# Scratch layout of split queries and keys in a fused attention block: each hi and lo row stored once, and a head's operand put together by two loads in place of one

## Chip, cores, metric

One NeuronCore of a Trainium2 chip. The metric is the device time of one execution, in microseconds (us); several executions are measured, and the median counts.

## What is computed

A block of a transformer with conditioned layer norm (adaLN), batch 1, S = 2048 tokens, D = 512, H = 32 heads of 16 dims, hidden width F = 1792, all in fp32:

```python
mod = (silu(c) @ w_mod).reshape(1, 6, 1, 512)          # sa, ca, ga, sb, cb, gb
h = layernorm(x) * (1 + ca) + sa
q, k, v = split(h @ wqkv)                              # 32 heads of 16
p = softmax(einsum("bhqd,bhkd->bhqk", q, k) * 16**-0.5)
x = x + ga * ((p @ v) @ wo)
h = layernorm(x) * (1 + cb) + sb
t = h @ w1 + b1
out = x + gb * ((t * tanh(softplus(t))) @ w2)          # Dense, Mish, Dense
```

## The kernel before

**Split products.** TensorE (PE) multiplies in a reduced fp32 form, so a number a is kept as hi(a), rounded, and lo(a) = a − hi(a), and a product is made as hi·hi + lo·hi + hi·lo. For the scores this sum is made by the contraction itself: a head has 16 dims, and each dim takes three rows, q rows (hi, hi, lo) against k rows (hi, lo, hi). That is 48 rows, and two more carry the negated row maximum of the softmax, in two parts, so a head's operand has 50 rows for q and 48 for k and lies in a field of 64 partitions. Two heads (a *pair*) share one buffer: head 0 on partitions 0 to 63, head 1 on 64 to 127. There are NR = 5 buffers `qa` [128, 512] and NR = 5 buffers `ka` [128, 2048], used in turn: pair pp takes buffer pp % 5.

**Scratch.** The q and k units (`qk_unit`) compute 128 columns of q or k (8 heads) for 512 tokens, split them into `qh` and `ql` (in the first stage on ACT and DVE, later on GpSimd, lines L98 and L101), and store both into DRAM: `kscr` [32 heads, 48, 2048] and `qscr` [32, 50, 2048], in the very row order that the operand has. So a hi row is stored twice: for q by two of three transfers of 256 KB (L272), for k by one transfer of 512 KB (L276) beside one of 256 KB for the low rows (L277). The two rows for the maximum are zeros from `constants()`. A pair's loads are then one transfer for each head: `load_q` (L313) reads 50 consecutive rows of 2 KB, `load_k` (L322) 48 rows of 8 KB. Pairs 0 and 1, which come first, take 48 rows of q, and k in pieces of 512 tokens.

**Attention.** 4 blocks of 512 queries times 8 groups of 4 heads are 32 iterations n; an iteration has pairs 2n and 2n+1 and 16 steps of 128 keys. A step has 4 score products (L588) with their exponentials on ACT (L591), 8 products p·v (L606), 4 products for the maxima (L539), each reduced on DVE (L541), and parts of other work: the remaining q, k and v units and later the second half of the block (L139, L132). The maxima of iteration n run 20 steps ahead of its scores; the first ones, before there are scores, run at L553 and L555 while qkv is still being made. When those of an iteration are done, `max_rows` turns them (L568), splits them into `mt` on DVE (L571), and four small transfers (L577, `qa<-mt`) put them into rows 48 and 49 of the heads' `qa`; the first score of that iteration waits for them. At an iteration's end the sums of the softmax go to another layout (L631, `sm<-ot`), DVE takes their reciprocals (L641), and these go out to DRAM and come back spread over partitions (L642, L644); four more transfers move the heads' outputs (L635).

**Order.** The order of all engines is written out by the program. A step t has two half steps, numbered h = 2t and 2t+1, and `at(h, f)` puts f there. Pairs 2 and 3 are loaded at h = −22 and −8, pair 4 at h = 17; from then on odd pairs 2n+1 at 32(n−1), which is 8 half steps ahead of their first maximum, and even ones earlier, at 32(n−2) and 2, 9 or 15 more (the first for n = 3, 4, 5 and 7). All transfers are issued by one engine, SyncE (SP), strictly in program order; each one, beside the waits for its data, waits until the transfer issued eight before it has landed (eight completion counters, DMAHW0 to DMAHW7, taken in turn). So at most eight are under way, and a transfer that waits holds up all behind it.

Of the kernel before, what the change touches and what calls it, by code (L numbers as in the profile page):

```python
# [8 lines left out]
F32 = mybir.dt.float32  # L9
# [9 lines left out]
def adaln_block(ctx: ExitStack, tc: tile.TileContext, x, wqkv, wo, w1, b1, w2, c, w_mod, out):  # L19
    nc = tc.nc  # L20
    P = 128
    S, D = x.shape[1], x.shape[2]
    F = w1.shape[1]
    H = 32
    DH = D // H
    DK = D // P
    FT = F // P
    TB = 512
# [25 lines left out]
    dram = ctx.enter_context(tc.tile_pool(name="dram", bufs=1, space=DRAM))  # L54
    ps = ctx.enter_context(tc.tile_pool(name="ps", bufs=1, space=PSUM))

    kscr = dram.tile([H, 48, S], F32, name="kscr")
    qscr = dram.tile([H, 50, S], F32, name="qscr")
    vscr = dram.tile([G, P, VROW], F32, name="vscr")
    woscr = dram.tile([DK, P, 2, D], F32, name="woscr")  # L60
    w1scr = dram.tile([FT, P, 2, D], F32, name="w1scr")
# [27 lines left out]
    def dap(t, off, ap):  # L89
        return bass.AP(tensor=t.tensor, offset=t.offset + off, ap=ap)  # L90

    def hi_copy(eng, hi, src):
        if eng == "a":
            nc.scalar.copy(hi, src)
        elif eng == "v":
            nc.vector.tensor_copy(hi, src)
        else:
            nc.gpsimd.tensor_scalar(hi, src, 1.0, 0.0, op0=ALU.mult, op1=ALU.add)  # L98

    def lo_sub(eng, lo, src, hi):  # L100
        (nc.gpsimd if eng == "p" else nc.vector).tensor_sub(lo, src, hi.bitcast(F32))  # L101
# [15 lines left out]
    def mm3(acc, ah, al, bh, bl, late="a"):  # L117

        n = len(ah)
        seq = ((ah, bh), (ah, bl), (al, bh)) if late == "a" else ((ah, bh), (al, bh), (ah, bl))  # L120
        seq = [(l[k], r[k]) for l, r in seq for k in range(n)]
        for i, (l, r) in enumerate(seq):
            mm(acc, l, r, i == 0, i == len(seq) - 1)
# [41 lines left out]
    def bank(tag="ms"):  # L165
        return ring() if tag == "ring" else ps.tile([P, TB], F32, tag=tag, name="bk", bufs=1)
# [25 lines left out]
    def clear(h):  # L192

        return h if h < 60 or h % 32 < 25 else h - h % 32 + 34
# [10 lines left out]
    def at(h, f):  # L205

        hooks.setdefault(h, []).append(f)
# [38 lines left out]
    def qk_unit(kind, ct, tb, tag):  # L246

        wh, wl = slices[kind, ct]
        acc = bank(tag)
        ts_ = slice(tb * TB, (tb + 1) * TB)  # L250
        mm3(acc, [wh[:, k, :] for k in range(DK)], [wl[:, k, :] for k in range(DK)],
            [h_h[:, k, ts_] for k in range(DK)], [h_l[:, k, ts_] for k in range(DK)], "b")

        def fin(h=None):
            qh = qp.tile([P, TB], F32R, tag="qh", name="qh", bufs=2)
            ql = qp.tile([P, TB], F32R, tag="ql", name="ql", bufs=2)
            if h is None:
                hi_copy("a", qh, acc)
                lo_sub("v", ql, acc, qh)
            else:  # L260
                qf = pw.tile([P, TB], F32, tag="raw", name="qf", bufs=1)
                nc.scalar.copy(qf, acc)  # L262
                hi_copy("p", qh, qf)
                lo_sub("p", ql, qf, qh)
            scr, rows = (qscr, 50) if kind == 0 else (kscr, 48)

            def put():
                put_away.add((kind, ct, tb))
                o = 8 * ct * rows * S + tb * TB
                if kind == 0:  # L270
                    for r, src in enumerate((qh, qh, ql)):
                        nc.sync.dma_start(dap(scr, o + r * S, [[rows * S, 8], [3 * S, DH], [1, TB]]), src.bitcast(F32))  # L272
                    return
                hi = qh.bitcast(F32)
                twice = bass.AP(tensor=hi.tensor, offset=hi.offset, ap=[list(hi.ap)[0], [0, 2], [1, TB]])
                nc.sync.dma_start(dap(scr, o, [[3 * S, P], [2 * S, 2], [1, TB]]), twice)  # L276
                nc.sync.dma_start(dap(scr, o + S, [[3 * S, P], [1, TB]]), ql.bitcast(F32))  # L277

            put() if h is None else at(clear(h + (5 if h > 60 else 2)), put)
        return fin  # L280
# [25 lines left out]
    def load_q(pp, rows=50):  # L306
        n, j = divmod(pp, 2)
        qb, g = divmod(n, G)
        h = 4 * g + 2 * j
        qt = qa[pp % NR].bitcast(F32)  # L310
        assert (0, h // 8, qb) in put_away, (pp, put_away)
        for s in range(2):
            nc.sync.dma_start(qt[64 * s:64 * s + rows, :], qscr[h + s, :rows, qb * TB:(qb + 1) * TB])  # L313

    def load_k(pp, tb=None):
        n, j = divmod(pp, 2)
        h = 4 * (n % G) + 2 * j
        kt = ka[pp % NR].bitcast(F32)
        at_ = slice(0, S) if tb is None else slice(tb * TB, (tb + 1) * TB)
        assert {(1, h // 8, i) for i in (range(NB) if tb is None else (tb,))} <= put_away, (pp, put_away)  # L320
        for s in range(2):
            nc.sync.dma_start(kt[64 * s:64 * s + 48, at_], kscr[h + s, :, at_])  # L322

    def load_pair(pp):
        load_q(pp)
        load_k(pp)


    with ExitStack() as es:
# [23 lines left out]
        zer = lp.tile([P, TB], F32, name="zer")  # L353
# [113 lines left out]
        apply_tb(1)  # L467
        def constants():
            for q4 in range(S // TB):
                nc.sync.dma_start(dap(qscr, 48 * S + q4 * TB, [[50 * S, H], [S, 2], [1, TB]]), zer[:64, :])  # L470
            nc.sync.dma_start(dap(vscr, VROW - 16, [[VROW, P], [P * VROW, G], [1, 16]]), zer[:, :16 * G])
            nc.sync.dma_start(b1c, b1.rearrange("(f p) -> p f", p=P))

        def unit(fin):
            pe_run()
            fin()

        constants()
        for tb in range(NB):
            if tb + 2 < NB:  # L480
# [27 lines left out]
            if tb == 0:  # L508
                for pp in range(2):
                    load_q(pp, 48)  # L510
            for pp in range(2):
                load_k(pp, tb)
# [7 lines left out]
    ap = ctx.enter_context(tc.tile_pool(name="ap", bufs=1, reuse_waits="tile"))  # L520
# [1029 lines left out]
```

## Time and profile before

| | |
|---|---|
| measured times | 1690.85, 1691.66, 1695.13 us; median 1691.66 |
| profiled execution | 1691.02 us, of it 1689.2 us span of instructions (1.8 around it) |
| busy share | PE 99%, DVE 85%, ACT 80%, GpSimd (POOL) 49% |
| granted TensorE clock | 1.000 |
| transfers | 238.98 MB, mean 141 GB/s |
| share of chain that ended last | PE 91%, DVE 3%, ACT 3%, DMA 2% |

Rows of a timeline give the start and the duration in us, the engine and line, what is written from what (`qa<-qscr`: from qscr into qa), how many neighbours a row gathers (x4), and in brackets the idle time before it and what ended that. An SP row spans the issuing, not the data's way; when the data has landed shows only where somebody waits for it. Rows of the waits give the total in us, the number of times, and the longest. Rows of windows give the busy time of PE, PE's weight loads (PEld), DVE, ACT and POOL with the number of instructions, the granted clock, the share of time in which the 16 DMA engines moved packets, and GB/s.

### The profile page before, as it was taken

To read this page: it belongs to the slowest core of one execution; us is meant where nothing else is said; L and a number is where in the kernel's file an instruction comes from. 1 tells how busy PE (TensorE), PEld (TensorE's weight loads), DVE (VectorE), ACT (ScalarE), POOL (GpSimd) and SP (SyncE) were. 2 spreads that over 40 slices of the span, in tenths; PEclk is the share of its full clock that TensorE was granted. 3 is DMA by queue.
4 is the path that set the end of the run, shared out by engine and by line. 5 is a ranking of instruction groups with operands and counts; after the bars stand their busy time and mean duration, and the time that the engine had idled before them with its cause. 6 is when DMAs were issued, how large, how long until landed. Compare 5 with 4: busy or idle time off the path is not lost.

```text
span 1689.2 us, 33772 instructions
## 1 busy us (share of the span) xinstructions
PE 1667.3 (99%) x12418; PEld 921.5 (55%) x12418; DVE 1441.5 (85%) x2369; ACT 1355.1 (80%) x2612; POOL 821.1 (49%) x843
## 2 busy tenths in 40 slices
PE   7999999999999999999999999999999999999999
PEld 5755655555444455555555455555555455555687
DVE  8898888888989988888889888888889888883377
ACT  6257777777778998888888998888888998889674
POOL 7555224655313564556323564556323565555442
PEclk9999999999999999999999999999999999999999
DMA  7877556777755443434355434534354533533261
GB/s 248 269 244 199 147 150 185 218 223 216 231 142 146 110 94 98 117 88 129 84 137 152 115 77 93 139 77 127 87 144 122 130 94 77 144 107 132 75 230 63
DMA packets 115406, 238.98 MB, mean 141 GB/s; under 512 B 24928, under 2 KB 50544, under 8 KB 109288
## 3 DMA queue, kind: packets, MB, share of 16 engines
q1 hardware_dynamic: 115240, 236.82, 49.9%
q8 instruction: 98, 1.61, 0.4%
q14 instruction: 68, 0.56, 0.1%
HBM read 180.48 MB, written 51.45 MB: 137 GB/s over the span
## 4 chain that ended last, share of the span: by engine, by line
PE 91%; DVE 3%; ACT 3%; DMA 2%; POOL 1%; issue 1%; SPq 0%; ACTq 0%; DVEq 0%; POOLq 0%
PE bk L606 29%; PE ring L588 22%; PE ring L539 20%; PE bk L139 11%; PE bk L132 3%; PE ring L1219 2%; PE ring L132 2%; DVE mx L541 2%; ACT pr L591 1%; PE ring L553 0%; DMA qa<-mt 0%; DMA xt<-in_A_x 0%; PE ring L922 0%; DMA kscr<-qh 0%; PE ring L568 0%
## 5 line engine op out<-in xcount | busy, mean ns | idle before, releaser
L541 DVE TENSOR_REDUCE mx<-ring 128x1 f32<-128x512 f32 x1968 | 1223.1, 682 | 150.0 <-PE ring L539 136.4
L591 ACT ACTIVATE pr<-ring 128x512 f32<-128x512 f32 x2048 | 1078.4, 603 | 207.1 <-PE bk L139 124.7
L539 PE MATMUL ring<-ka,qa 64*128 64x512 f32 x1968 | 817.9, 429 | 1.4 <-ACT pr L591 1.1
L588 PE MATMUL ring<-qa,ka 64*128 64x512 f32 x2048 | 759.1, 402 | 3.4 <-ACT pr L591 1.9
L606 PE MATMUL bk<-pr,vg 128*32 128x512 f32 x4096 | 545.1, 604 | 0.0
L539 PEld LDWEIGHTS ring<-ka,qa 64*128 64x128 f32 x1968 | 350.5, 184 | 326.2 <-DVE mx L541 251.3
L588 PEld LDWEIGHTS ring<-qa,ka 64*128 64x128 f32 x2048 | 373.7, 184 | 194.7 <-DVE mx L541 111.4
L139 PE MATMUL bk<-h,w 64*128 64x512 f32 (+1 forms) x1080 | 278.1, 390 | 0.0
L139 PE MATMUL bk<-w,a_h 64*128 64x512 f32 x632 | 210.9, 413 | 0.0
L139 PEld LDWEIGHTS bk<-h,w 64*128 64x128 f32 x1080 | 178.5, 184 | 9.3 <-ACT pr L591 1.5
L606 PEld LDWEIGHTS bk<-pr,vg 128*32 128x32 f32 x4096 | 81.2, 108 | 135.4 <-issue 126.0
L139 PE MATMUL bk<-w,a_l 64*128 64x512 f32 x316 | 124.0, 392 | 0.0
L139 PEld LDWEIGHTS bk<-w,a_h 64*128 64x128 f32 x632 | 106.8, 184 | 4.3 <-ACT hb L800 1.0
L978 POOL TENSOR_TENSOR y<-yd,y 128x512 f32<-128x512 f32 x44 | 56.9, 1293 | 89.0 <-ACT yd L977 79.7
L812 POOL TENSOR_SCALAR qq<-ee 128x512 f32<-128x512 f32 x25 | 15.5, 619 | 169.6 <-ACT ee L806 169.6
L828 POOL TENSOR_TENSOR qq<-qq,rr 128x512 f32<-128x512 f32 x42 | 54.1, 1289 | 85.9 <-ACT rr L822 85.9
L814 POOL TENSOR_TENSOR hb<-hb,ee 128x512 f32<-128x512 f32 x42 | 54.1, 1288 | 79.6 <-DVE ee L810 77.7
L139 PE MATMUL bk<-w,o_hl 64*128 64x512 f32 x288 | 79.1, 405 | 0.0
L101 POOL TENSOR_TENSOR a_l<-hb,a_h 128x512 fp32r<-128x512 f32 x53 | 73.1, 1379 | 4.4
L98 POOL TENSOR_SCALAR qh<-qf 128x512 fp32r<-128x512 f32 x27 | 16.7, 619 | 90.8 <-ACT qf L262 69.4
L139 PEld LDWEIGHTS bk<-w,a_l 64*128 64x128 f32 x316 | 58.3, 185 | 3.4
L139 PE MATMUL bk<-h_h,wl 64*128 64x512 f32 x168 | 57.2, 420 | 0.2 <-ACT pr L591 0.2
(219 smaller groups left out, 1909.1 us busy)
## 6 DMA issues: line engine op xcount, KB each, us to landing
ka<-kscr SPq DMA_DIRECT2D x124, 384.0 KB
w<-w2scr SPq DMA_DIRECT2D x56, 512.0 KB
w<-w1scr SPq DMA_DIRECT2D x46, 512.0 KB
vg<-vscr SPq DMA_DIRECT2D x32, 552.0 KB
qa<-qscr SPq DMA_DIRECT2D x124, 100.0 KB
kscr<-qh SPq DMA_DIRECT2D x16, 512.0 KB
qscr<-qh SPq DMA_DIRECT2D x32, 256.0 KB
w2scr<-hl SPq DMA_DIRECT2D x14, 512.0 KB
```

What stands on the lines that cost most here:

```text
L101: (nc.gpsimd if eng == "p" else nc.vector).tensor_sub(lo, src, hi.bitcast(F32))
L132: nc.tensor.matmul(acc, l, r, start=start, stop=stop)
L139: i = nc.tensor.matmul(acc, l[64 * g:64 * g + 64], r[64 * g:64 * g + 64], start=start and not then, stop=bool(stop and then))
L539: nc.tensor.matmul(pm, qt[64 * s:64 * s + 64, qs * P:(qs + 1) * P], kt[64 * s:64 * s + 64, kb * TB:(kb + 1) * TB], start=True, stop=True)
L541: nc.vector.tensor_reduce(out=mxs[n][:, s, 4 * j + qs, kb:kb + 1], in_=pm, op=ALU.max, axis=AX.X)
L588: nc.tensor.matmul(p_, kt[64 * s:64 * s + 64, kc * P:(kc + 1) * P], qt[64 * s:64 * s + 64, :], start=True, stop=True)
L591: e = nc.scalar.activation(pr, p_, AF.Exp, scale=SCALE)
L606: nc.tensor.matmul(accs[n][32 * h:32 * h + 32, :], vgs[n][:, o:o + 32], pts.pop((t, h)), start=(kc == 0), stop=(kc == 15))
L814: (nc.vector if tail else nc.gpsimd).tensor_mul(hb, hb, ee)
L828: nc.gpsimd.tensor_mul(qq, qq, rr)
L978: nc.gpsimd.tensor_add(y[i], yd, y[i])
L1219: nc.tensor.matmul(po[i // 2][:, i % 2, :], l[:, s], w[:, r, :], start=(f == 0 and j == 0), stop=(f == FT - 1 and j == 2))
```

## The change

Each hi and each lo row is stored once, two rows for a dim: `kscr` is [32, 32, 2048] and `qscr` [32, 34, 2048] (rows 32 and 33 are the zeros). A unit's stores are two transfers of 256 KB, for q and for k alike. A head's operand is put together by two loads. For q the operand has rows hi (16), then hi and lo in turn (32), then the zeros: the first transfer reads 34 consecutive rows (32 for pairs 0 and 1) to partitions 16 and up, the second the 16 hi rows to partitions 0 to 15. For k the first transfer reads each hi row twice (32 rows), the second the 16 lo rows. What is computed stays the same, and so do the bytes that are loaded; the row order within the contraction differs, for q and k alike.

```diff
-    kscr = dram.tile([H, 48, S], F32, name="kscr")
-    qscr = dram.tile([H, 50, S], F32, name="qscr")
+    kscr = dram.tile([H, 32, S], F32, name="kscr")
+    qscr = dram.tile([H, 34, S], F32, name="qscr")
...
-                if kind == 0:
-                    for r, src in enumerate((qh, qh, ql)):
-                        nc.sync.dma_start(dap(scr, o + r * S, [[rows * S, 8], [3 * S, DH], [1, TB]]), src.bitcast(F32))
-                    return
-                hi = qh.bitcast(F32)
-                twice = bass.AP(tensor=hi.tensor, offset=hi.offset, ap=[list(hi.ap)[0], [0, 2], [1, TB]])
-                nc.sync.dma_start(dap(scr, o, [[3 * S, P], [2 * S, 2], [1, TB]]), twice)
-                nc.sync.dma_start(dap(scr, o + S, [[3 * S, P], [1, TB]]), ql.bitcast(F32))
+                for r, src in enumerate((qh, ql)):
+                    nc.sync.dma_start(dap(scr, o + r * S, [[rows * S, 8], [2 * S, DH], [1, TB]]), src.bitcast(F32))
...
-            nc.sync.dma_start(qt[64 * s:64 * s + rows, :], qscr[h + s, :rows, qb * TB:(qb + 1) * TB])
+            b, o = 64 * s, (h + s) * 34 * S + qb * TB
+            nc.sync.dma_start(qt[b + DH:b + rows, :], dap(qscr, o, [[S, rows - DH], [1, TB]]))
+            nc.sync.dma_start(qt[b:b + DH, :], dap(qscr, o, [[2 * S, DH], [1, TB]]))
...
-            nc.sync.dma_start(kt[64 * s:64 * s + 48, at_], kscr[h + s, :, at_])
+            b, o = 64 * s, (h + s) * 32 * S + at_.start
+            nc.sync.dma_start(kt[b + DH:b + 48, at_], dap(kscr, o, [[2 * S, DH], [0, 2], [1, w]]))
+            nc.sync.dma_start(kt[b:b + DH, at_], dap(kscr, o + S, [[2 * S, DH], [1, w]]))
```

In `constants()` the zeros go to rows 32 and 33. Over the whole program SP issues 1274 transfers in place of 1022: 128 more for q, 140 more for k, 16 fewer stores. The order of the instructions on DVE, ACT and POOL is the same, and so is that of PE, save that the products that start on freshly loaded buffers wait for more completion counters (118 more such waiting instructions). After the stores, line numbers are 2 lower (L575 for L577, L629 for L631, and so on), the loads stand at L308, L309, L319 and L320.

The first place that matters is on SP, ahead of the first four puts of the maxima: the loads of pair 3 and one k unit's stores. Before (`qa_110` and `ka_631` are pair 3's buffers, `qa_107` and `qa_108` those of pairs 0 and 1; in brackets what a row waits for, DMAHW being the completion counters):

```order
L313 DMA qa_110<-qscr 50x512 [waits DMAHW5_49]
L313 DMA qa_110<-qscr 50x512 [waits DMAHW6_49]
L322 DMA ka_631<-kscr 48x2048 [waits DMAHW7_49]
L322 DMA ka_631<-kscr 48x2048 [waits DMAHW0_49]
L276 DMA kscr<-qh 128x2x512 [waits DMAHW1_49,Pool_49]
L277 DMA kscr<-ql 128x512 [waits DMAHW2_49,Pool_49]
L577 DMA qa_107<-mt 2x4x128 [waits DMAHW3_49,DVE_49,PE_49]
L577 DMA qa_108<-mt 2x4x128 [waits DMAHW4_49,PE_49]
```

The same place in the changed program:

```order
L308 DMA qa_110<-qscr 34x512 [waits DMAHW3_49]
L309 DMA qa_110<-qscr 16x512 [waits DMAHW4_49]
L308 DMA qa_110<-qscr 34x512 [waits DMAHW5_49]
L309 DMA qa_110<-qscr 16x512 [waits DMAHW6_49]
L319 DMA ka_650<-kscr 32x1x2048 [waits DMAHW7_49]
L320 DMA ka_650<-kscr 16x2048 [waits DMAHW0_49]
L319 DMA ka_650<-kscr 32x1x2048 [waits DMAHW1_49]
L320 DMA ka_650<-kscr 16x2048 [waits DMAHW2_49]
L271 DMA kscr<-qh 128x512 [waits DMAHW3_49,Pool_49]
L271 DMA kscr<-ql 128x512 [waits DMAHW4_49,Pool_49]
L575 DMA qa_107<-mt 2x4x128 [waits DMAHW5_49,DVE_49,PE_49]
L575 DMA qa_108<-mt 2x4x128 [waits DMAHW6_49,PE_49]
```

The first put stands six rows behind pair 3's first load before and ten behind it now; the load of pair 2, further up, has four more in the same way, and one store of q less lies between. From pair 2's first load to the first put SP has 25 transfers before and 32 now.

The second place is on SP too, at the end of iteration 0: the loads of pair 6, a q unit's stores, a small store, and the transfer of the sums (L631). Before:

```order
L313 DMA qa_108<-qscr 50x512 [waits DMAHW4_49]
L313 DMA qa_108<-qscr 50x512 [waits DMAHW5_49]
L322 DMA ka_106<-kscr 48x2048 [waits DMAHW6_49]
L322 DMA ka_106<-kscr 48x2048 [waits DMAHW7_49]
L272 DMA qscr<-qh 8x16x512 [waits DMAHW0_49,Pool_49]
L272 DMA qscr<-qh 8x16x512 [waits DMAHW1_49]
L272 DMA qscr<-ql 8x16x512 [waits DMAHW2_49,Pool_49]
L730 DMA mscr<-gate_99 4x128 [waits DMAHW3_49,Activation_49]
L631 DMA sm<-ot 128x1x16 [waits DMAHW4_49,Activation_49]
```

And now:

```order
L308 DMA qa_108<-qscr 34x512 [waits DMAHW6_49]
L309 DMA qa_108<-qscr 16x512 [waits DMAHW7_49]
L308 DMA qa_108<-qscr 34x512 [waits DMAHW0_49]
L309 DMA qa_108<-qscr 16x512 [waits DMAHW1_49]
L319 DMA ka_106<-kscr 32x1x2048 [waits DMAHW2_49]
L320 DMA ka_106<-kscr 16x2048 [waits DMAHW3_49]
L319 DMA ka_106<-kscr 32x1x2048 [waits DMAHW4_49]
L320 DMA ka_106<-kscr 16x2048 [waits DMAHW5_49]
L271 DMA qscr<-qh 8x16x512 [waits DMAHW6_49,Pool_49]
L271 DMA qscr<-ql 8x16x512 [waits DMAHW7_49,Pool_49]
L728 DMA mscr<-gate_99 4x128 [waits DMAHW0_49,Activation_49]
L629 DMA sm<-ot 128x1x16 [waits DMAHW1_49,Activation_49]
```

The sums' transfer stood eight rows behind the first load of pair 6 and stands eleven behind it now: four loads more, one store less.

More of the change, by code (lines that the diff above doesn't have):

```diff
@@ L264, in fin @@
                 lo_sub("p", ql, qf, qh)
-            scr, rows = (qscr, 50) if kind == 0 else (kscr, 48)
+            scr, rows = (qscr, 34) if kind == 0 else (kscr, 32)
             def put():
@@ L318, in load_k @@
         kt = ka[pp % NR].bitcast(F32)
-        at_ = slice(0, S) if tb is None else slice(tb * TB, (tb + 1) * TB)
+        at_, w = (slice(0, S), S) if tb is None else (slice(tb * TB, (tb + 1) * TB), TB)
         assert {(1, h // 8, i) for i in (range(NB) if tb is None else (tb,))} <= put_away, (pp, put_away)
         for s in range(2):
-            nc.sync.dma_start(kt[64 * s:64 * s + 48, at_], kscr[h + s, :, at_])
+            b, o = 64 * s, (h + s) * 32 * S + at_.start
+            nc.sync.dma_start(kt[b + DH:b + 48, at_], dap(kscr, o, [[2 * S, DH], [0, 2], [1, w]]))
+            nc.sync.dma_start(kt[b:b + DH, at_], dap(kscr, o + S, [[2 * S, DH], [1, w]]))
     def load_pair(pp):
@@ L469, in constants @@
             for q4 in range(S // TB):
-                nc.sync.dma_start(dap(qscr, 48 * S + q4 * TB, [[50 * S, H], [S, 2], [1, TB]]), zer[:64, :])
+                nc.sync.dma_start(dap(qscr, 32 * S + q4 * TB, [[34 * S, H], [S, 2], [1, TB]]), zer[:64, :])
             nc.sync.dma_start(dap(vscr, VROW - 16, [[VROW, P], [P * VROW, G], [1, 16]]), zer[:, :16 * G])
```

## Prediction

> **What bounds the kernel now.** The page's span, its busy times and its chain come first: they tell which engine a delay must reach before it counts.
>
> ```profile
> span 1689.2 us, 33772 instructions
> PE 1667.3 (99%) x12418; PEld 921.5 (55%) x12418; DVE 1441.5 (85%) x2369; ACT 1355.1 (80%) x2612; POOL 821.1 (49%) x843
> PE 91%; DVE 3%; ACT 3%; DMA 2%; POOL 1%; issue 1%; SPq 0%; ACTq 0%; DVEq 0%; POOLq 0%
> ```
>
> PE is the bound nearly everywhere, so a transfer costs time only where PE, or DVE ahead of it, ends up waiting for it. The waits, asked for PE, show where PE's products now wait for a transfer:
>
> ```profile
> PE ring L588 <- DMA qa<-mt: 1.2, 1, 1.2
> ```
>
> One wait of 1.2 us, for the maxima's put. The change therefore can take away hardly anything, and the question is where it adds. The windows tell how full the transfers' side is (the last two columns: DMA share, GB/s):
>
> ```profile
> 28.00:62.00 34.00, 32.28 (x206) 25.30 (x205) 30.02 (x38) 18.34 (x32) 19.52 (x19) 1.00 0.58 191
> 60.00:70.00 10.00, 10.00 (x73) 8.00 (x72) 9.18 (x9) 1.49 (x4) 4.76 (x6) 1.00 0.92 283
> 80.00:90.00 10.00, 10.00 (x46) 6.18 (x45) 9.24 (x9) 2.17 (x4) 6.53 (x8) 1.00 0.98 340
> 110.00:200.00 90.00, 90.00 (x827) 53.24 (x824) 77.76 (x131) 69.69 (x143) 43.31 (x36) 1.00 0.59 164
> ```
>
> From 60 to 90 us the DMA engines are full (0.92 and 0.98); before that and from 110 on they are at 0.58 and 0.59. That early stage is where more transfers can hurt first. The SP timeline of it:
>
> ```profile
> 71.28 1.19 SPq L313 DMA_DIRECT2D qa<-qscr  x2
> ...
> 88.84 2.49 SPq L313 DMA_DIRECT2D qa<-qscr  x2
> 91.37 1.11 SPq L322 DMA_DIRECT2D ka<-kscr  x2
> ...
> 93.06 0.41 SPq L277 DMA_DIRECT2D kscr<-ql  x1
> 94.67 2.98 SPq L577 DMA_DIRECT2D qa<-mt  x4
> ```
>
> Pair 2 is loaded from 71.28, pair 3 from 88.84, and the first four puts follow from 94.67 to 97.65. PE takes the first score soon after:
>
> ```profile
> 101.88 0.49 PE L588 MATMUL ring<-qa,ka 64*128 64x512 f32 x1
> ```
>
> **The change, part by part.**
>
> *Bytes.* A head's loads still bring 48 rows of k and 50 of q; only stores fall.
>
> ```profile
> DMA packets 115406, 238.98 MB, mean 141 GB/s; under 512 B 24928, under 2 KB 50544, under 8 KB 109288
> ...
> ka<-kscr SPq DMA_DIRECT2D x124, 384.0 KB
> qa<-qscr SPq DMA_DIRECT2D x124, 100.0 KB
> kscr<-qh SPq DMA_DIRECT2D x16, 512.0 KB
> qscr<-qh SPq DMA_DIRECT2D x32, 256.0 KB
> ```
>
> Each of 16 k units and 16 q units stores 256 KB less: 8.4 MB of 238.98. Between 71 and 95 us lie three such units, 768 KB, at the 340 GB/s of the window 2.3 us of transfer time. Whether this comes back is part of A's lower bound.
>
> *A: the first puts.* Between pair 2's first load (71.28) and the first put (94.67) SP has 25 issues now and 32 afterwards: four more for each of two pairs, one store less. SP issues 25 in 23.4 us, 0.94 us each; seven more are 6.6 us. SP had no work from 93.47 (93.06 + 0.41) to 94.67, where the put waited for its data: 1.2 us of slack come off, 5.4 remain. The score at 101.88 comes 4.2 us after the last put left SP (97.65). How long a put takes to land I read where PE did wait for one (the puts on SP's timeline, the score on PE's):
>
> ```profile
> 371.83 3.34 SPq L577 DMA_DIRECT2D qa<-mt  x4
> 380.46 0.47 PE L588 MATMUL ring<-qa,ka 64*128 64x512 f32 x1 [1.24 <-DMA qa<-mt]
> ```
>
> There 5.3 us lay between the last issue (375.17) and the score. So the 4.2 us at the first puts hold no slack worth naming, and I take **+5.5 us**. Upper bound: seven issues at the pace of pair 3's q loads (2.49 / 2 = 1.25), no slack, 8.7. Lower: half-sized transfers free their counters sooner and the seven cost nothing, 0. The pace of pair 2's loads (1.19 / 2 = 0.60) lies between; I stay near 0.94, since it is the mean of this very stretch. PE, full in these windows, can't make the time up.
>
> Why SP is slow there, the waits of its queue show: loads held by earlier stores.
>
> ```profile
> SPq L313 <- DMA qscr<-ql: 10.4, 4, 5.0
> SPq L322 <- DMA kscr<-ql: 6.9, 3, 3.3
> ```
>
> A q store, written as 8 × 16 rows, held it up to 5.0 us, a k store of 128 rows 3.3. [...]
>
> *B: pair 4*, used 12 steps after the first score. The step is the distance of two p·v groups:
>
> ```profile
> 751.41 1.06 PE L606 MATMUL bk<-pr,vg 128*32 128x512 f32 x8
> 754.24 1.06 PE L606 MATMUL bk<-pr,vg 128*32 128x512 f32 x8
> ```
>
> 2.83 us, so at 101.88 + 34.0 = 135.9.
>
> ```profile
> 124.75 0.80 SPq L313 DMA_DIRECT2D qa<-qscr  x2
> 125.59 0.78 SPq L322 DMA_DIRECT2D ka<-kscr  x2
> ```
>
> How long a large transfer takes at worst, the chain shows, in the full stage (start and duration):
>
> ```profile
> 92.58 7.33 DMA kscr<-qh
> ```
>
> Four issues end at 126.4; with 7.33 us to land they are there by 133.7, 2.2 early. Eight issues take 1.6 more, and those ahead of it can bring 1 or 2: **+0.7**, 0 to 2.
>
> *C: the sums of iteration 0*, on SP's timeline, and their reciprocal on DVE's (last row):
>
> ```profile
> 149.43 1.38 SPq L313 DMA_DIRECT2D qa<-qscr  x2
> ...
> 157.35 0.57 SPq L272 DMA_DIRECT2D qscr<-ql  x1
> 160.17 0.52 SPq L730 DMA_DIRECT2D mscr<-gate  x1
> 160.96 0.60 SPq L631 DMA_DIRECT2D sm<-ot  x1
> ...
> 168.19 0.24 DVE L641 RECIPROCAL rc<-sm 128x16 f32<-128x16 f32 x1
> ```
>
> From pair 6's first load (149.43) to the sums (160.96) are 8 issues in 11.5 us, 1.44 each; three more are 4.3. SP sat idle from 157.92 to 160.17, 2.25, which comes off: 2.1. The reciprocal is 6.6 us behind the sums' issue, some of which is slack: **+1.5**, 0 to 4. DVE waits there with all its reductions behind it, and PE for those.
>
> *D: the same in later iterations.* There the sums' transfer waits for ACT, not for a counter:
>
> ```profile
> SPq L631 <- ACT pr L591: 110.3, 26, 7.8
> ```
>
> 26 of the 31 are of this kind, 4.2 us each, more than four issues of an undisturbed load (0.8 / 2 each, row 125.59): mostly covered; **+0.5**, 0 to 2.
>
> *E: the wait at 380*, behind q stores that get fewer: **−0.7**, between 0 and −1.2.
>
> *F: longer waits on PE.* 118 more of these rows:
>
> ```profile
> L539 PEldq EVENT_SEMAPHORE  x122: 51/51/51, 111.8 to 1512.2; - x122
> ```
>
> They exist now from 111.8 on, and from 110 to 200 PE is busy 90.00 of 90 all the same: the wait runs beside the products before it. **0**; without that cover 118 × 51 ns = 6.0 us.
>
> *G: steady loads of odd pairs* are issued four steps, 11.3 us, ahead of use, and later ones with light traffic:
>
> ```profile
> 751.26 0.67 SPq L313 DMA_DIRECT2D qa<-qscr  x2
> 751.98 0.78 SPq L322 DMA_DIRECT2D ka<-kscr  x2
> ```
>
> 1.5 us of issuing become 3.0; with 7.33 landed after 10.3: **0**, covered by 1 us.
> *H: pairs 0 and 1*, loaded ahead of 60 us, k in four pieces of 512 tokens: 20 more issues (4 for q, 16 for k). The groups of first maxima show when the pieces are wanted:
>
> ```profile
> 52.86 0.73 PE L553 MATMUL ring<-ka,qa 64*128 64x512 f32 x4
> ...
> 55.38 0.73 PE L553 MATMUL ring<-ka,qa 64*128 64x512 f32 x4
> ```
>
> A group comes every 2.5 us, 20 of them up to the first score, and the last piece isn't needed by the first twelve, 30 us. 20 issues at 0.4 (row 125.59) are 8 us, spread over 34 us in which the DMA engines stand at 0.58: **0**; if a third fell on the first maximum, 2.7.
>
> Sum: 5.5 + 0.7 + 1.5 + 0.5 − 0.7 = **+7.5 us** (ends, without F and H: −1.2 and +16.7). The span becomes 1696.7, the profiled run 1691.02 + 7.5 = 1698.5. That run lay 0.64 below the median of 1691.66, so for the median I say **1699.2**.
>
> **Rivals.**
>
> *Bytes set the pace, not issues* (ends on the other side: not slower). The engines are at 0.98 and the bytes ahead of the puts fall. If 32 smaller transfers leave as fast as their bytes, the puts go out at 94.67 as before. It decides at a pace of 24.6 / 32 = 0.77 us per issue or less. A is 0, B and C near 0.7 together: −1 to +4, about 1693.7. For it: 283 GB/s at 0.92, so the limit is not the bytes alone but also the packets, whose number in loads stays. Against it: each issue in the timeline waits for one particular landing, and the pair 3 loads took 0.55 to 1.25 each even behind large stores.
>
> *Fewer bytes win.* The wait at 380 goes (1.24) and the 2.3 us of stores come back ahead of the scores: −3.5, 1688.2. Against it: PE is at 10.00 of 10.00 until 90 us, and there is no wait to take away.
>
> *Every odd pair late.* If issue to landing exceeds the 11.3 us (10.3 by G), each of 30 odd pairs holds PE: 1 us late each gives +30, 1729. For it: G's cover is only 1 us. Against it: 7.33 was taken at 340 GB/s, and the whole span's mean is 141.
>
> *The change doesn't do what it says*: the loads move the same bytes with more issues, so for them nothing is saved; this is in the sum.
>
> **How the numbers follow.** Forecast (SP issues bind early, +4 to +17): 0.70. Bytes set the pace: 0.17. Fewer bytes win: 0.05. Odd pairs late: 0.08. From the second case's middle, 1692, to the first case's upper end, 1709, leaves out the fourth, the third and parts of the others, 0.2 together. About 0.3%, 5.1 us, is what a measurement of this kernel can tell from no change: faster is below 1686.6, slower above 1696.7. Slower: 0.65 of the forecast's 0.70, and 0.08: 0.73. Faster: 0.02, the far end of the third case. The same: the rest, 0.25.
>
> **What would show it.** Right: the first score waits for `qa<-mt`, some 5 us, at about 107; the first put leaves SP near 100; near 170 the reciprocal waits for `sm<-ot`; from 200 on the distance of like steps from before stays constant. A wrong: no wait for `qa<-mt` there. G wrong: waits of L539 for `ka<-kscr` in every iteration, and the time above 1709. F wrong: a span longer by some us without any wait for a transfer. Wrong altogether: below 1692, with SP's pace under 0.77 us.

## Result and the profile after

| | before | after |
|---|---|---|
| median of the runs | 1691.26 us | 1714.62 us |
| ratio | | 1.0134, 95% interval 1.0116 to 1.0152 |
| profiled execution, span | 1691.02, 1689.2 us | 1716.85, 1715.0 us |
| granted TensorE clock, mean | 1.000 | 0.993 |

The changed kernel is 23.4 us slower, three times the forecast of 7.5 and beyond its range. Its page, with the granted clock in 40 slices (43 us each):

```profile
span 1715.0 us, 34146 instructions
PE 1674.0 (98%) x12418; PEld 924.4 (54%) x12418; DVE 1442.1 (84%) x2369; ACT 1355.8 (79%) x2612; POOL 822.0 (48%) x843
PEclk9989999999999999999999999999999999999999
PE 85%; DMA 6%; DVE 3%; ACT 2%; SPq 2%; issue 1%; POOL 1%; ACTq 0%; POOLq 0%; DVEq 0%
```

Transfers now hold 6% of the chain that ended last in place of 2%, and the third slice no longer has the full clock. PE's waits show the mechanism that was forecast, and several that were not:

```profile
PE ring L586 <- DMA qa<-mt: 6.5, 2, 5.4
PE ring L586 <- DVE mx L539: 4.4, 3, 2.0
PE ring L551 <- DVE mt L569: 2.0, 1, 2.0
PE ring L537 <- DMA ka<-kscr: 1.5, 1, 1.5
PE bk L132 <- POOL wl L101: 1.3, 1, 1.3
```

Both programs run the same 12418 products in the same order, so the start of each product can be compared one by one. How much later it starts than before, in us (columns: the product's time in the trace of before; "score" is the first score at 101.88 with the product ahead of it; the rows below "after" are experiments told further down):

| | 80 | 95 | ahead of score | score | 120 | 140 | 180 | 350 | 500 | 900 | 1680 |
|---|---|---|---|---|---|---|---|---|---|---|---|
| after | 0.0 | 2.2 | 8.4 | 13.9 | 15.1 | 16.3 | 18.8 | 19.6 | 21.3 | 25.0 | 25.5 |
| 34 + 16 rows on before | 0.0 | 0.0 | 0.3 | 7.6 | 8.9 | 10.1 | 16.7 | 16.9 | 25.5 | 27.4 | 28.6 |
| 32 + 18 rows on before | −0.1 | −0.1 | −0.1 | 1.7 | 3.0 | 3.0 | 3.0 | 3.1 | 4.9 | 5.1 | 6.2 |
| 32 + 18 rows on after | −0.1 | 0.8 | 1.4 | 5.7 | 9.0 | 8.9 | 9.0 | 8.9 | 7.5 | 7.5 | 7.8 |
| 20 tiny transfers on before | 0.0 | 0.0 | 0.0 | 3.1 | 7.4 | 7.3 | 7.4 | 7.5 | 8.2 | 8.1 | 8.1 |

So 15.1 of 25.5 us are lost by 120 us, and the rest in steps. Three things made the first part. SP falls behind before 70 us. Before, four k loads of pairs 0 and 1 and, at the end of that stage, the load of a weight slice stand on its timeline so:

```profile
39.46 1.76 SPq L322 DMA_DIRECT2D ka<-kscr  x4
60.63 0.45 SPq L234 DMA_DIRECT2D wr<-in_A_wqkv  x1
```

After, the first and last of eight, and the weight slice:

```profile
39.55 0.64 SPq L319 DMA_DIRECT2D ka<-kscr  x1
43.97 0.58 SPq L320 DMA_DIRECT2D ka<-kscr  x1
68.77 0.42 SPq L234 DMA_DIRECT2D wr<-in_A_wqkv  x1
```

Eight take 5.0 us (39.55 to 44.55) in place of 1.76: twice as many, and each longer. The weight slice goes out 8.1 us later. GpSimd, which prepares weights from the transfers behind it, waits 9.7 us longer, in two rows of its waits up to 90 us, before and after:

```profile
POOL ep L98 <- DMA ep<-in_B_w: 6.8, 1, 6.8
```

```profile
POOL ep L98 <- DMA ep<-in_B_w: 16.5, 1, 16.5
```

That delay reaches PE at 82 us (`wl`, the row of PE's waits above). Second, from pair 2's first load to the puts:

```profile
80.69 0.72 SPq L308 DMA_DIRECT2D qa<-qscr  x1
102.29 0.30 SPq L308 DMA_DIRECT2D qa<-qscr  x1
112.13 2.86 SPq L575 DMA_DIRECT2D qa<-mt  x4
```

Pair 2 starts 9.4 us late (71.28 before), and its first load to the first put takes 31.4 us for 32 issues, 0.98 each, 8.1 more than before. What SP waited for is in the chain (start, duration):

```profile
81.83 9.63 DMA qa<-qscr
103.01 9.04 DMA qa<-qscr
112.96 2.66 DMA qa<-mt
```

Two of the q loads, 68 KB each, took over 9 us, longer than any large transfer named in the prediction. Third, PE waits, and its clock goes down (the column before the last two):

```profile
115.76 0.76 PE L586 MATMUL ring<-qa,ka 64*128 64x512 f32 x1 [5.43 <-DMA qa<-mt]
```

```profile
95.00:100.00 5.00, 4.12 (x18) 2.43 (x16) 1.52 (x2) 0.10 (x1) 0.00 (x0) 1.00 0.85 263
100.00:105.00 5.00, 2.97 (x7) 1.47 (x8) 4.28 (x5) 1.28 (x3) 3.10 (x4) 0.71 0.79 272
105.00:110.00 5.00, 5.00 (x16) 3.07 (x14) 2.85 (x3) 0.59 (x1) 1.90 (x3) 0.61 0.95 171
110.00:115.00 5.00, 0.33 (x2) 0.00 (x0) 0.10 (x1) 0.00 (x0) 0.24 (x1) 0.73 0.41 120
115.00:120.00 5.00, 3.83 (x17) 2.60 (x19) 3.16 (x5) 2.70 (x5) 2.12 (x3) 0.58 0.71 217
120.00:125.00 5.00, 4.77 (x35) 2.68 (x35) 4.44 (x8) 4.57 (x9) 3.09 (x4) 1.00 1.01 300
```

By finer windows the clock is at 0.50 from 102.1 to 108.9 and from 112.4 to 119.1, and at 1.00 between. The first dip lies ahead of the score and, by the chain above, cost nothing of its own: the put was held by the q load that landed at 112.0, and PE, slow or not, had to wait for the put. Behind the score the distance grows by 1.2 us, from 13.9 to 15.1.

After 120 us the steps come from pair 4's loads (1.1 us), from iterations' ends, where DVE's reciprocal waits for the sums with all reductions behind it, and once from an odd pair's k loads. DVE's timeline at iteration 0 and later, and PE's at 880 us:

```profile
187.29 0.25 DVE L639 RECIPROCAL rc<-sm 128x16 f32<-128x16 f32 x1 [2.68 <-DMA sm<-ot]
375.33 0.25 DVE L639 RECIPROCAL rc<-sm 128x16 f32<-128x16 f32 x1 [2.48 <-DMA sm<-ot]
883.82 0.25 DVE L639 RECIPROCAL rc<-sm 128x16 f32<-128x16 f32 x1 [0.75 <-DMA sm<-ot]
```

```profile
880.09 0.55 PE L537 MATMUL ring<-ka,qa 64*128 64x512 f32 x1 [1.47 <-DMA ka<-kscr]
```

SP's waits name the holder there too: its transfer of the reciprocals, L640, was held 12 times by a q load.

```profile
SPq L640 <- DMA qa<-qscr: 21.1, 12, 3.2
```

### The profile page after: what moved, and what is told of

The parts are those of the page before. It is cut to its first block, busy times and chain, and to the rows that moved or that the text cites. A ratio compares the mean times of both kernels' runs of the same rounds, so it can differ in the third digit from the quotient of the medians.

```text
span 1715.0 us, 34146 instructions
## 1 busy us (share of the span) xinstructions
PE 1674.0 (98%) x12418; PEld 924.4 (54%) x12418; DVE 1442.1 (84%) x2369; ACT 1355.8 (79%) x2612; POOL 822.0 (48%) x843
## 4 chain that ended last, share of the span: by engine, by line
PE 85%; DMA 6%; DVE 3%; ACT 2%; SPq 2%; issue 1%; POOL 1%; ACTq 0%; POOLq 0%; DVEq 0%
PE bk L604 27%; PE ring L586 20%; PE ring L537 18%; PE bk L139 11%; PE ring L1217 2%; DMA qa<-qscr 2%; PE ring L132 2%; DVE mx L539 2%; PE bk L132 2%; ACT pr L589 1%; DMA ka<-kscr 1%; DMA qscr<-qh 1%; DMA qa<-mt 1%; DMA sm<-ot 1%; DMA xt<-in_A_x 0%
## 5 line engine op out<-in xcount | busy, mean ns | idle before, releaser
L586 PE MATMUL ring<-qa,ka 64*128 64x512 f32 x2048 | 761.4, 403 | 13.2 <-DMA qa<-mt 6.5
L586 PEld LDWEIGHTS ring<-qa,ka 64*128 64x128 f32 x2048 | 374.4, 184 | 205.3 <-DVE mx L539 119.1
L139 PEld LDWEIGHTS bk<-h,w 64*128 64x128 f32 x1080 | 178.6, 184 | 10.1 <-ACT pr L589 1.5
L812 POOL TENSOR_TENSOR hb<-hb,ee 128x512 f32<-128x512 f32 x42 | 54.1, 1289 | 79.6 <-DVE ee L808 77.6
```

The costliest lines, as they stand in the source:

```text
L139: i = nc.tensor.matmul(acc, l[64 * g:64 * g + 64], r[64 * g:64 * g + 64], start=start and not then, stop=bool(stop and then))
L586: nc.tensor.matmul(p_, kt[64 * s:64 * s + 64, kc * P:(kc + 1) * P], qt[64 * s:64 * s + 64, :], start=True, stop=True)
L812: (nc.vector if tail else nc.gpsimd).tensor_mul(hb, hb, ee)
```

## Experiments

Two theories: I, the number of SP's issues; R, the rows of the q loads. Changes to time are against the kernel before in the same series.

**34 and 16 rows on the kernel before.**

```diff
-            nc.sync.dma_start(qt[64 * s:64 * s + rows, :], qscr[h + s, :rows, ...])
+            for lo, hi in ((16, rows), (0, 16)):
+                nc.sync.dma_start(qt[64 * s + lo:64 * s + hi, :], qscr[h + s, lo:hi, ...])
```

> The kernel before, its storage and its k loads untouched, with each q load of 50 rows cut into 34 and 16 rows (32 and 16 for pairs 0 and 1). Theory I (the number of transfers that SP issues before the first scores sets the delay): 4 transfers more ahead of 60 us and 4 for pairs 2 and 3, 8 of the 28 less stores that the change adds there, so 2 to 6 us slower, 1694 to 1698. Theory R (a load of 34 rows lands late and holds its completion counter, as the 9.6 and 9.0 us in the changed kernel's chain suggest): most of the change's loss is here already, 12 to 20 us slower, 1704 to 1712, with q loads of pairs 2 and 3 that take 9 us to land.

1716.4 us, ratio 1.0157 (1.0142 to 1.0172): 25.8 slower, more than the whole change (23.4), and beyond what either theory asked for. The wait for the puts is there:

```profile
PE ring L589 <- DMA qa<-mt: 11.2, 3, 7.3
```

The table shows the loss at the first score and again at 180 and 500 us. Theory R stands, if it is the 34 rows and not the 128 further loads (32 and 18 rows, below, decide that). Of theory I this says nothing.

**k loads in two on the kernel before.**

```diff
-            nc.sync.dma_start(kt[64 * s:64 * s + 48, at_], kscr[h + s, :, at_])
+            for lo, hi in ((16, 48), (0, 16)):
+                nc.sync.dma_start(kt[64 * s + lo:64 * s + hi, at_], kscr[h + s, lo:hi, at_])
```

> The kernel before, its storage and its q loads untouched, with each k load of 48 rows cut into 32 and 16 rows. Theory I: 16 transfers more ahead of 60 us, 4 for pairs 2 and 3, so most of the change's loss, 12 to 20 us slower, 1704 to 1712, and pair 2's loads begin some 7 us later than before (71.3 us). Theory R: 0 to 5 us slower, 1691 to 1696.

1703.2, ratio 1.0078 (1.0063 to 1.0093), 12.6 slower, the lower end of what theory I asked for. Pair 2 is loaded from 77.6, 6.3 late. So issues cost too, where no load has 34 rows. The first eight halves on SP's timeline are issued in 0.45 us each, where the change's eight, stepped or with rows repeated, took 0.63:

```profile
39.53 3.61 SPq L323 DMA_DIRECT2D ka<-kscr  x8
```

**The changed kernel without 34-row loads.**

```diff
-    qscr = dram.tile([H, 34, S], F32, name="qscr")
+    qscr = dram.tile([H, 36, S], F32, name="qscr")
...
+            nc.sync.dma_start(qt[b:b + 32, :], dap(qscr, o, [[S, 32], [1, TB]]))
+            nc.sync.dma_start(qt[b + 32:b + rows, :], dap(qscr, o, [[2 * S, rows - 32], [1, TB]]))
...
```

> The changed kernel with the operand's rows in another order, so that a head's q is loaded as 32 rows (hi and lo in turn) and 18 rows (hi, and the two zeros, which lie two rows apart in a field of 36), k as 32 and 16; the number of transfers, their order and nearly all bytes are those of the changed kernel, only no load has 34 rows. Theory I: as slow as the changed kernel, 20 to 25 us above before, 1711 to 1716. Theory R: 12 to 20 us faster than the changed kernel, 1695 to 1703, and pair 2's q loads land within 6 us.

1699.85, ratio 1.0059 (1.0042 to 1.0076): 9.2 above before, 14.8 below the changed kernel's median (14.2 by each one's distance from its own before). The same number of transfers, in the same order. Pair 2's first load, the puts, and the first score:

```profile
80.13 0.80 SPq L308 DMA_DIRECT2D qa<-qscr  x1
102.83 2.84 SPq L575 DMA_DIRECT2D qa<-mt  x4
```

```profile
107.62 0.76 PE L586 MATMUL ring<-qa,ka 64*128 64x512 f32 x1 [4.26 <-DMA qa<-mt]
```

32 issues now take 22.7 us, 0.71 each: less than the 23.4 that 25 took before. So without the 34-row loads the issues of pairs 2 and 3 cost nothing (the prediction's rival "bytes set the pace" had its point at 0.77), and all of the 8.2 us by which the puts are late was there at pair 2's first load, 8.9 late, from the issues ahead of 70 us. Nor does anything come later: the table stands at 9.0 at 120 us, and falls by 1.3 at 380, where the old wait goes, as term E of the prediction had it. Pair 2's q loads had landed within 4.6 us, inside the 6 expected (80.13 to 81.71 on SP's timeline; the transfers eight behind them, which wait for their counters, left at 84.72 to 86.16), and SP's waits for q loads at L640 are nearly gone:

```profile
SPq L640 <- DMA qa<-qscr: 1.3, 1, 1.3
```

**20 tiny transfers on the kernel before.**

```diff
+        nc.sync.dma_start(dmy[i:i + 1, :], x[i:i + 1, :16])   # behind each load of pairs 0 and 1
```

> The kernel before with one transfer of 64 bytes, which nobody waits for, behind each of the 20 loads of pairs 0 and 1: the 20 more issues of the early stage without any other part of the change. Theory I: SP loses 20 times 0.4 us, pair 2 is loaded 7 to 9 us later than at 71.3 us, and since the first scores' puts stand behind that on SP, the kernel is 6 to 10 us slower, 1697 to 1701. Theory R: the stage has room for them, 0 to 1 us, 1691 to 1692.

1696.7, ratio 1.0039 (1.0024 to 1.0054), 6.0 slower. Theory I holds; pair 2 came 4.8 late in place of 7 to 9, as one tiny transfer takes SP some 0.33 us (63.13 to 63.45 on its timeline), less than the 0.45 of a half of a k load (above).

```profile
76.08 1.18 SPq L321 DMA_DIRECT2D qa<-qscr  x2
98.51 3.59 SPq L589 DMA_DIRECT2D qa<-mt  x4
```

```profile
105.01 0.76 PE L600 MATMUL ring<-qa,ka 64*128 64x512 f32 x1 [3.08 <-DMA qa<-mt]
```

```profile
105.00:110.00 5.00, 4.10 (x15) 2.42 (x15) 2.63 (x4) 2.37 (x5) 3.48 (x4) 0.50 0.97 303
110.00:115.00 5.00, 4.71 (x21) 3.31 (x22) 3.34 (x5) 3.17 (x7) 0.32 (x2) 0.50 1.02 357
```

PE waited 3.1 us and was 7.4 late at 120 us: the wait was followed by 10 us at half the clock.

**32 and 18 rows on the kernel before.** As the first experiment, with `((0, 32), (32, rows))`.

> The kernel before with each q load of 50 rows cut into 32 and 18 rows (32 and 16 for pairs 0 and 1): as many transfers as in the run with 34 and 16, the same bytes, only no 34-row load. Theory R (a 34-row load is slow by its row count): 0 to 5 us above before, 1690 to 1696, where 34 and 16 gave 1716. Rival (it is the 128 further loads as such): 1710 to 1718 again.

1698.3, ratio 1.0046 (1.0031 to 1.0061), 7.2 slower: 2 us more than expected, but 18 us less than 34 and 16. Its clock stayed at 1.00; half of the rise (table) is at the first score, and the rest, in small steps at 380 and 427 us and later, stays unexplained.

**Work in place of the wait.** On the kernel without 34-row loads:

```diff
+        if t == 0:
+            for _ in range(20):
+                nc.tensor.matmul(ring_t[:, ring_at[0] % NRING, :], h_h[:, 0, :P], h_h[:, 0, :TB], start=True, stop=True)
```

> The kernel with 32- and 18-row q loads and stores of the change (1699.9), with 20 further products, which nobody reads, on TensorE ahead of the first score, where it waited 4.3 us for the maxima's put. Theory C (the wait costs more than its length, since the clock stands at 0.50 to 0.68 for some 8 us behind it): no dip of the granted clock behind the first score, and 3 to 5 us less, 1695 to 1697. Rival (the dip has another cause, or the further products only fill the wait): 1699 to 1701, the clock as it was.

1697.2, ratio 1.0039 (1.0025 to 1.0053), 2.7 faster than without (3.1 by each one's distance from its own before); for the 3 to 5 expected a little small. Without the products, and with them, where the clock kept its full value:

```profile
105.00:110.00 5.00, 2.38 (x12) 1.80 (x14) 1.54 (x3) 1.33 (x3) 1.89 (x2) 0.68 0.84 264
110.00:115.00 5.00, 4.71 (x21) 3.10 (x19) 3.16 (x5) 2.81 (x6) 1.89 (x2) 0.50 0.96 289
```

```profile
105.00:110.00 5.00, 5.00 (x28) 3.43 (x27) 1.34 (x3) 1.63 (x4) 2.15 (x3) 1.00 0.86 262
110.00:115.00 5.00, 4.29 (x32) 2.83 (x28) 4.97 (x9) 4.34 (x9) 2.32 (x3) 1.00 0.96 287
```

So the dip is an answer to PE's idleness, and here it cost some 3 us behind a wait of 4.3.

**The first puts from ACT's queue.** On the same kernel:

```diff
-                    nc.sync.dma_start(
+                    (nc.scalar if n == 0 else nc.sync).dma_start(
                         qa[(2 * n + j) % NR][64 * s + 48:64 * s + 50, :]...
```

> The kernel with 32- and 18-row q loads and stores of the change (1699.9), with the first four puts of the maxima issued by ACT's queue in place of SP's, so that they stand behind none of SP's further issues and wait only for their own completion counters. Theory I (what is left of the loss is SP's lateness at these puts): the wait of the first score falls from 4.3 us to under 2, and the time to 1691 to 1695. Rival (the puts wait for landings, whoever issues them): 1698 to 1701.

1702.5, ratio 1.0069 (1.0054 to 1.0084): not faster but 2.6 slower than without (2.2 by each one's distance from its own before), so theory I in its narrow form (only the puts are late) is refuted. The puts went out early, and the next late thing took their place; ACT's timeline, and PE's:

```profile
96.79 3.22 ACTq L575 DMA_DIRECT2D qa<-mt  x4
100.13 0.58 ACT L262 COPY qf<-bk 128x512 f32<-128x512 f32 x1 [3.74 <-DMA qa<-mt]
111.50 0.58 ACT L262 COPY qf<-bk 128x512 f32<-128x512 f32 x1 [8.10 <-POOL ql L101]
```

```profile
112.64 0.79 PE L537 MATMUL ring<-ka,qa 64*128 64x512 f32 x1 [6.59 <-ACT pr L589]
```

A k unit's copy on ACT waits for GpSimd's `ql`. GpSimd had waited 6.7 us, up to 109.5, for the store of an earlier `qh`, which SP issued at 104.2, behind pair 3's loads. The exponentials queue behind the copy. With the puts on SP the same copy stood at 108.67, 1 us behind the score that waited for the put, and the store at 101.9. The 2.3 us between the two stores are about the loss: the early puts took completion counters that SP's loads of pair 3 were to use next, and one of these loads waited 1.2 us for a put. SP's lateness has more than one exit.

**The k part alone.** q is stored three times in the change's row order and loaded by one transfer of 50 rows, k as in the changed kernel:

```diff
+                if kind == 0:
+                    for r, step, src in ((0, 1, qh), (DH, 2, qh), (DH + 1, 2, ql)):
+                        nc.sync.dma_start(dap(scr, o + r * S, [[rows * S, 8], [step * S, DH], [1, TB]]), src.bitcast(F32))
+                    return
```

> The change's k part alone: k stored once and loaded by two transfers, q stored three times in the change's row order and loaded by one transfer of 50 rows. If parts act alone and the 34-row loads carry most of the loss: 1699 to 1704 (9 to 13 us above before, as the k loads cut in two gave 12.6, less what the k stores save). If the k part's repeated reads of hi rows cost something by themselves: above 1706.

1700.6, ratio 1.0065 (1.005 to 1.008), 9.5 slower, in the first band: the repeated reads and the fewer stores together make no difference that shows beside the 12.6 of the loads cut in two (the intervals overlap); one may hide the other.

**The second transfers of pairs 0 and 1 on ACT's queue**, on the kernel without 34-row loads:

```diff
-            nc.sync.dma_start(kt[b + 32:b + 48, at_], ...)
+            (nc.scalar if pp < 2 else nc.sync).dma_start(kt[b + 32:b + 48, at_], ...)   # and q alike
```

> The kernel with 32- and 18-row q loads and stores of the change (1699.9), with the second transfer of each load of pairs 0 and 1 (20 of them, ahead of 70 us) issued by ACT's queue, so that SP has no more issues there than before. Theory I with early issues as the larger part (20 tiny transfers alone gave 6.0 us): pair 2's loads begin at 72 to 74 us in place of 80, the first score waits at most 2 us for the put, 1691 to 1695. Rival (the 8 further transfers of pairs 2 and 3, right ahead of the puts, weigh more; or the completion counters, which both queues share, hold either queue alike): 1697 to 1701.

1703.6, ratio 1.007 (1.0055 to 1.0085): a miss. PE waited earlier, for ACT, which could not copy PE's results while it issued; ACT's and PE's timelines:

```profile
36.17 2.21 ACTq L320 DMA_DIRECT2D ka<-kscr  x4
```

```profile
39.86 0.50 PE L132 MATMUL ring<-h_h,wh 128*128 128x512 f32 x1 [3.13 <-ACT h_h L438]
```

By 60 us on before's scale PE was 13.2 late: two waits of 3.1 and 3.0 us, and behind each, for 6 to 7 us, four products of 128x256 took 1.05 to 1.23 us in place of 0.64. Nothing was added later; with PE that late, no wait for the puts was left, so the run can't say how large the early issues are. The expectation had left ACT's own work out.

**And those of pairs 2 and 3** (`pp < 4`).

> As the run with the second transfers of pairs 0 and 1 on ACT's queue, and those of pairs 2 and 3 too: SP issues no load more ahead of the first scores than before, and three stores of q and none of k fewer. Theory I: no wait of the first score worth naming, the wait at 380 us gone, so 1689 to 1692. Rival (ACT, held by these transfers, copies later units later and TensorE waits there): 1694 to 1702.

1702.2, ratio 1.0071 (1.0054 to 1.0088). The rival holds, at its upper end: 9.4 us lost by 60 us at the same places.

**17 and 33 rows on the kernel before.** As the first experiment, with `((0, 17), (17, rows))` (16 and 32 rows for pairs 0 and 1).

> The kernel before with each q load of 50 rows cut into 17 and 33 rows (16 and 32 for pairs 0 and 1): again as many transfers and bytes as with 34 and 16 (1716.4) or 32 and 18 (1698.3). [...] Rival (34 rows were slow for their bytes, 68 KB in place of 64, or for beginning at partition 16): 1696 to 1701.

1725.1, ratio 1.0197 (1.0174 to 1.0221): 33.4 slower, worse than 34 and 16, and far above the rival's 1696 to 1701. The same bytes, the same number of transfers; only where the cut lies differs: 7 us for 32/18, 26 for 34/16, 33 for 17/33.

```profile
PE ring L589 <- DMA qa<-mt: 13.7, 4, 8.1
```

No run came below the kernel before, and none pointed to a version that would.

## Why the prediction was wrong

**The direction and the place were right:** the first score waits for `qa<-mt`, 5.4 us against 5.5; the puts are late through SP's order; the reciprocal waits for the sums near 187, where 2.5 us are lost (C: 1.5); pair 4 costs 1.1 (B: 0.7); stored bytes bring nothing early.

**A's number agrees by luck.** The pace of 0.98 us per issue against 0.94 is not the price of an issue: with as many issues and no 34-row load it was 0.71. A took the wait at the score for the whole loss there, while PE was by then 8.4 late already. It also said that the 4.2 us between the last put and the score hold no slack. In the changed kernel the score follows 0.8 us behind the last put (112.13 + 2.86 to 115.76), so some 3.5 us were slack; the first put is 17.5 us late and the score 13.9. And the two rows of SP's waits that A read as holding the loads there belong to the stage before, H's: between 71 and 96 us no load waited for a store, while up to 72 us the kernel before has:

```profile
SPq L322 <- DMA kscr<-ql: 6.9, 3, 3.3
SPq L313 <- DMA qscr<-ql: 5.0, 1, 5.0
```

**H failed.** The 20 issues ahead of 60 us were put at 0, "covered", because DMA engines stood at 0.58 and the last k piece is not needed for 30 us. The cover looked at the wrong party. The pieces were in time; what was late was SP itself, and all that it issues in order behind: weights for GpSimd, pair 2, pair 3, the puts. SP lost 8.1 us by the weight slice and never got them back before the score. The prediction's own estimate of the issues, 8 us, was right; charging nothing for them was not. By themselves (20 tiny transfers) they cost 6.0 us; the changed kernel without 34-row loads, where the puts' lateness is theirs alone, loses 9.2.

**The rows of a load had no term in the forecast**, and A's upper end lay only 3.2 us above it. Taking the 34-row loads out of the changed kernel gives 14.8; putting them into the kernel before costs 25.8, of which 32/18 rows have 7.2. The traces of before and after hold several completion records for each load: 16 for one of 16, 32 or 48 rows, 11 for one of 50, 3 for one of 34 (of 11 and of 3 the first comes 0.5 and 0.4 us behind the issue). The last one is taken as the landing. Median issue to landing after 520 us: 3.1 us for 50 rows (before), 5.4 for 34 (after), though the latter has fewer bytes, 68 KB in place of 100; in the first stage the changed kernel's four loads of 32 rows, for pairs 0 and 1, took 2.0 to 2.4. A k load of 32 rows behind 34-row loads needed 7.4, where before one of 48 rows, 384 KB in place of 256, needed 6.5; the prediction did not think of that. Its 16 records, each at its median, tell more: 14 are there by 5.35 us, the last two at 7.0 and 7.4. Of the 16-row q loads' 16, 14 are there by 3.1, the last two at 4.7 and 5.5, as late as the 34-row loads' own two at 4.6 and 5.4. So a slow load holds its own counter, and of a load behind it two of 16 records come late. What these share with it the trace does not name, and why 17 and 33 rows are slower still was not shown.

**D and E** follow from that. Later iterations were put at +0.5; they cost 6.7 (18.8 at 180 us to 25.5), most of it in steps of 0.7, 2.0 and 3.5 at 262, 354 and 857 us on before's scale. The last step begins with the k load's wait; from 880.4 to 883.7 in its own time the clock stands at 0.50 behind it. E's gain of 0.7 came only where there were no 34-row loads (1.3). Without them in the changed kernel D is about 0. The sum without F's 6.0 us was right: between the steps PE's distance from before stays constant, so it pays nothing for the further counters.

**A term was missing: the clock.** Before, the granted clock was 1.00 up to the span's last 2 us. In the changed kernel it stood at 0.50 from 102.1 to 108.9, behind a gap of PE of 2.0 us that ended at 101.1; from 112.4 to 119.1, around the end (115.8) of one of 5.4; and from 880.4 to 883.7, behind one of 1.5 that ended at 880.1. Gaps of 2.0 us at 188 and 1.9 at 376 left it at 1.00. In the experiments the lowest window of 5 us, at the end of a gap or behind it, has:

| | gap of PE, us | clock |
|---|---|---|
| 17 + 33 rows on before | 8.1 | 0.50 |
| 34 + 16 rows on before | 7.3 | 0.64 |
| first puts from ACT's queue | 6.6 | 0.59 |
| 32 + 18 rows on after | 4.3 | 0.50 |
| k loads in two on before | 3.1 | 0.50 |
| 20 tiny transfers on before | 3.1 | 0.50 |
| k loads in two on before, an earlier gap | 2.2 | 1.00 |
| k part alone | 2.1 | 0.58 |
| 32 + 18 rows on before | 1.7 | 1.00 |

In the changed kernel the clock was full again 3.4 to 7.8 us behind a gap's end, with the tiny transfers some 10. The table of the result gives what a dip costs at most, as the rise from the score to 120 us: 4.3 with the tiny transfers, 3.3 with 32 + 18 rows on after, but 1.2 in the changed kernel. There the windows from 100 to 110 and from 115 to 120 us lack 5 × (0.29 + 0.39 + 0.42) = 5.5 us of clock, most of it ahead of the score, where PE had to wait anyway. That the gap is the cause is shown for one place, where filling the wait with products kept the clock at 1.00. The prediction priced waits at their length.

Of its four cases none is the measured one: the forecast's mechanism is there at three times its size, and "bytes set the pace", refuted for the change as made, is what the changed kernel does between pair 2's load and the puts once the 34-row loads are gone. That the time lies in the early stage and not in every odd pair's loads (one wait, 1.5 us) spoke against the fourth rightly.

What stays open: the 25.8 of 34/16 alone and the 23.4 of the whole change, which holds 34 rows and 16 more early issues, don't add up from parts. That 14.8 and 9.2 make the whole is so by construction, since both are distances from the same run; 25.8 and 12.6, measured one by one, make far more. The table shows the losses overlapping at the first score, where only the latest of several late things counts, but whether the stores that the change saves gave something back was not separated.

## What to carry to other kernels

An engine that issues transfers in order is a resource with a timeline of its own: charge every further issue to all that stands behind it, up to the next point where it really idles, even if the transfer itself is early (20 tiny ones, which nobody waits for, cost 6.0 us here). Before counting bytes, try where a load's rows are cut: 32 and 18 in place of 34 and 16 or of 17 and 33 were worth 15 to 26 us here at nearly the same bytes. And add to a wait of PE the clock that may follow it, 0.50 behind waits of 3.1 and 4.3 us here and worth up to some 4 us where no other wait hides it, or give PE something to do.

## What was not expected of the hardware

- Where a load was cut outweighed its size: the same 50 rows cut 32/18, 34/16 or 17/33 made the same kernel 7, 26 and 33 us slower.
- A load of 34 rows of 2 KB took up to 9.6 us in a full stage. Of the 16 completion records of a k load behind such loads the last two came at 7.0 and 7.4 us, the other 14 by 5.35 (medians).
- SP needs longer for some issues than for others: 0.63 us for a piece of k with rows repeated or stepped, 0.45 for a plain one, of 48 rows or of 32 and 16.
- At or behind seven gaps of PE of 3.1 to 8.1 us the granted clock went down, to 0.50 to 0.64 over 5 us; three times a gap of 1.5 to 2.1 us was enough, and four times one of 1.7 to 2.2 was not.
